# Four early transfers and two stores of a convolution with a maxout layer behind it, put in another place

## The chip, the cores and the metric

The kernel runs on one core of one Trainium2 chip. The metric is the device time of one execution in microseconds (us). A core has engines that work side by side, each through its own queue in order: PE (TensorE, matrix products; its weight loads are listed as PEld), DVE (VectorE), ACT (ScalarE), POOL (GpSimd) and SP (SyncE). Here POOL and SP mostly issue transfers (DMAs), which then run on 16 DMA engines without them. An instruction waits at the head of its engine's queue until the semaphores that it needs have come; everything behind it on that engine waits too.

## The reference

```python
def _attn_ref(x, weight_gen):            # x: 8 x 4160 x 192, weight_gen: 8 x 4160 x 8 x 7
    w = weight_gen - np.max(weight_gen, axis=-1, keepdims=True)
    w = np.exp(w)
    w = w / (np.sum(w, axis=-1, keepdims=True) + 1e-09)
    ...                                  # x_unf: at each position the last 7 rows of x, by head
    out = np.einsum('bshk,bskhg->bshg', w, x_unf)

def _moe_ref(x, w1, w2, w_out):          # x: 33280 x 192, d_ff 1024
    h1 = x @ w1
    h2 = x @ w2
    g = np.maximum(h1, h2)
    return (g @ w_out).astype(np.float32)
```

First a dynamic convolution over seven positions, whose taps are a softmax over seven numbers for each position and head; then, on its result, two products with 192 x 1024 weights, their maximum, and a product back to 192 columns.

## The kernel before, in words

**Tiling.** The 33,280 rows lie on 128 partitions, 260 consecutive rows (columns, in the code) on each. Columns are handled in batches of 16, and a last one of 4. A batch needs its logits (`load_wg`, 448 KB), its rows of x in two halves of 8 columns (`load_x`, 384 KB each as they are read) and, ahead of them, the last six columns of the batch before, its halo (`load_halo`, 288 KB, a copy from one x buffer to the other). There are two x buffers and four buffers of logits, used in turn, so batch 2 writes into the x buffer of batch 0.

**Steps of a batch.** ACT takes the exponential of the logits (`exp_sum`, line 162), DVE sums them (`red`, 180), ACT takes the logarithm (`ln`, 186), DVE subtracts it (`shift`, 191), and ACT takes the exponential again, which gives the taps in bf16 (`weights`, 202). DVE multiplies x and taps (`mul`, 218) and adds the seven products (`adds`, 244, 250, 253). The result is transposed: for batches 0 and 1 by PE with an identity (`sum_part`, line 307, copied out by ACT in line 316), from batch 2 on by a DMA that SP issues (`transpose`, 262). PE computes the hidden layer as a difference of the two products (`hid_tile`, 362), ACT applies the relu (`relu`, 372), PE multiplies by the output weights and adds the linear part (402 and 415), and ACT copies the results to `o_t` (`evac`, 487), from which SP stores them (501).

**What sets the order.** The schedule is written by hand: an instruction's place on its engine is where the program writes it. PE's work is cut into tiles of 1024 hidden numbers, in groups of two and, from tile 16 on, three; `hidden(g, ...)` writes one group, and the steps of the softmax and convolution are written between groups (the table `early` for groups 3 to 7, the tables `NOW` and `AT` afterwards). `behind(first, load)` makes a load wait for a named instruction, mostly the relu of a tile (`relu_of`) or a copy of a transposed unit (`yt_of`), so that it takes its place among the transfers: the first half of batch 2 waits for relu 8, the second half for relu 14, the first half of batch 3 for relu 16, the third logits for the copies of the linear part's weights (`w10_of`), the fourth for the copy of unit 4. From the first transposition by DMA on, POOL reads one element of the transposed tile (`gate`, 270), and the next loads stand behind that.

**Stores.** `evac` makes one store when a unit of columns is full. A unit is four columns in batches 0 and 1, eight afterwards. A store is either written at once or put into a list `held`, which is emptied ahead of a later store or behind the next transposition. In the kernel before, the stores of units 0, 1 and 2 are written at once and those from unit 3 on are held.

Of the kernel before, what the change touches and what calls it, by code (L numbers as in the profile page):

```python
# [17 lines left out]
def _sub(base: bass.AP, off: int, dims):  # L18
    ap = [list(base.ap[0])] + [[int(s), int(c)] for s, c in dims]
    return dataclasses.replace(base, offset=base.offset + off, ap=ap)  # L20
# [3 lines left out]
def kernel(  # L24
# [9 lines left out]
    nc = tc.nc  # L34
# [71 lines left out]
    def actual(v):  # L106
        return v + 8 if v < LAST - 8 else v - (LAST - 8) if v < LAST else v

    def load_wg(b, eng, o=0, n=None):
        c0, w = BATCHES[b]  # L110
        if b not in wg_ts:
            wg_ts[b] = pwg.tile([P, w * WGC], FP32, name="wg_t", tag="wg")
        parts = [(o, n)] if n else [(0, 8), (8, 8)] if c0 + w == LAST else [(0, w)]
        for o, n in parts:
            load = eng.dma_start(
                out=wg_ts[b][:, o * WGC:(o + n) * WGC],
                in_=bass.AP(tensor=weight_gen.tensor, offset=actual(c0 + o) * WGC,
                            ap=[[CPP * WGC, P], [1, n * WGC]]),
            )
        return load  # L120

    def x_at(b, o):

        c = BATCHES[b][0] + o
        key, at = (b, o) if c < LAST - 8 else ("wrap", 0) if c < LAST else (NB - 2, 8)
        if key not in xb_ts:
            xb_ts[key] = pxb.tile([P, (16 + PAD) * D], BF16, name="xb_t", tag="xb")
        return xb_ts[key], at * D

    def load_x(b, o, n, halo=True):  # L130

        t, at = x_at(b, o)
        load = nc.gpsimd.dma_start(  # L133
            out=t[:, at + PAD * D:at + (PAD + n) * D],
            in_=bass.AP(tensor=x.tensor, offset=actual(BATCHES[b][0] + o) * D,
                        ap=[[CPP * D, P], [1, n * D]]),
        )
        if 0 < b < NB - 1 and o == 0 and halo:
            load_halo(b)
        if "wrap" in xb_ts and t is xb_ts["wrap"]:  # L140
            nc.gpsimd.memset(t[0:1, 0:PAD * D], 0.0)
            nc.gpsimd.dma_start(
                out=t[1:P, 0:PAD * D],
                in_=bass.AP(tensor=x.tensor, offset=(CPP - PAD) * D, ap=[[CPP * D, P - 1], [1, PAD * D]]),
            )
        return load
# [5 lines left out]
    def load_halo(b):  # L152

        nc.gpsimd.dma_start(out=x_at(b, 0)[0][:, 0:PAD * D],
                            in_=xb_ts[b - 1][:, 16 * D:(16 + PAD) * D])
# [8 lines left out]
    def part(b, i, of):  # L164

        n = BATCHES[b][1]
        h0, h1 = n * i // of * H, n * (i + 1) // of * H
        return slice(h0, h1), h0 * K, [[K, h1 - h0], [1, K]]
# [4 lines left out]
    def sums(b, hs):  # L173

        at = BATCHES[b][0] * H - (0 if b < FIRST else s_parts[0].shape[-1])
        return s_parts[b >= FIRST][:, at + hs.start:at + hs.stop]

    def red(b, i=0, of=1):
        hs, at, ap = part(b, i, of)
        nc.vector.reduce_sum(out=sums(b, hs), in_=_sub(e_ts[b], at, ap), axis=AX.X)  # L180

    def ln(b, i=0, of=1):
        if i == 0:
            s_ts[b] = psm.tile([P, BATCHES[b][1] * H], FP32, name="ln_t", tag="ln")
        hs = part(b, i, of)[0]
        nc.scalar.activation(out=s_ts[b][:, hs], in_=sums(b, hs), func=AF.Ln)  # L186
# [7 lines left out]
    def weights(b, o):  # L194

        w = dict(pieces(b))[o]
        if b not in en_ts:
            en_ts[b] = pen.tile([P, 16 * WGC * 2], BF16, name="en_t", tag="en")
        J = 2 if w == 4 and b < 2 else 1
        N = w * H // J  # L200
        for j in range(J):
            nc.scalar.activation(  # L202
                out=_sub(en_ts[b], (o * WGC + j * N * K) * 2, [[2 * N, K], [2, N], [1, 2]]),
                in_=_sub(wg_ts[b], (o * H + j * N) * K, [[1, K], [K, N], [0, 2]]), func=AF.Exp,
            )
# [79 lines left out]
    def sum_transpose(u, taps=range(K), amid=lambda: None, now=True):  # L285

        copy = sum_part(u, 0, 3, taps)
        amid()
        sum_part(u, 3, 6, taps)
        if now:  # L290
            copy()
        return copy
# [30 lines left out]
    relu_of, yt_of, w10_of = {}, {}, []  # L323

    def behind(first, load):

        tc.add_manual_dep(load.ins, first.ins.name, SYNC, reason="its place among the transfers")
# [3 lines left out]
    held = []  # L331
# [43 lines left out]
    def column(c):  # L375

        b = min(c // 16, NB - 1)
        for u, (ub, o, n) in enumerate(UNITS):
            if ub == b and o <= c - BATCHES[b][0] < o + n:
                k = c - BATCHES[b][0] - o  # L380
                return u, k // 2, k % 2

    def place(p):

        u, i, _ = column(2 * p)
        b, o, n = UNITS[u]
        return BATCHES[b][0] + o + i, n // 2
# [82 lines left out]
    def evac(p, n):  # L470

        tile_, at = op_at[p]
        o = o_t[0]
        if p == NT // 2 - 1:

            for j, (copy, eng) in enumerate(((nc.scalar.copy, nc.scalar), (nc.vector.tensor_copy, nc.sync))):
                copy(out=o_last[:, j * D:(j + 1) * D], in_=tile_[:, at + 512 * j:at + 512 * j + D])  # L477
                eng.dma_start(
                    out=bass.AP(tensor=out.tensor, offset=actual(place(p)[0] + 2 * j) * D, ap=[[CPP * D, P], [1, D]]),
                    in_=o_last[:, j * D:(j + 1) * D],  # L480
                )
            return
        runs = [[q for q in range(p, p + n) if column(2 * q)[0] == u]
                for u in range(column(2 * p)[0], column(2 * (p + n - 1))[0] + 1)]
        for qs in runs:
            c, h = place(qs[0])
            nc.scalar.copy(out=_sub(o, c % 24 * D, [[D, len(qs)], [h * D, 2], [1, D]]),  # L487
                           in_=_sub(tile_, at + (qs[0] - p) * D, [[D, len(qs)], [512, 2], [1, D]]))
        stores = []
        for q in range(p, p + n):  # L490
            u, i, _ = column(2 * q)
            if NU - 7 <= u < NU - 1 and i % 2:
                stores.append((nc.sync, place(q)[0] - 1, [4 * D, 2], [1, 2 * D]))
            elif u < NU - 7 and i == UNITS[u][2] // 2 - 1:
                stores.append((nc.sync, place(q)[0] - i, [1, 2 * (i + 1) * D]))
            if u == NU - 1:
                stores.append((nc.sync, place(q)[0], [2 * D, 2], [1, D]))
        for eng, c, *ap in stores:

            def issue(eng=eng, c=c, ap=ap, o=o):  # L500
                eng.dma_start(
                    out=bass.AP(tensor=out.tensor, offset=actual(c) * D, ap=[[CPP * D, P], *ap]),
                    in_=_sub(o, c % 24 * D, ap),
                )

            if 3 <= u < NU - 3:
                held.append(issue)
            else:
                while u > 3 and held:
                    held.pop(0)()  # L510
                issue()

# [14 lines left out]
    NU = len(UNITS)  # L527
# [88 lines left out]
    with tc.tile_pool(name="pstage", bufs=1) as pstage:  # L616
# [148 lines left out]
        def w10_copies(pw):  # L765

            nc.scalar.copy(out=_sub(w10, 0, [[D, 2], [1, D]]), in_=_sub(pw, 0, [[512, 2], [1, D]]))
            for to, frm, at in ((64, 0, 0), (0, 64, 512)):
                w10_of.append(nc.scalar.copy(out=w10[to:to + 64, 2 * D:3 * D],
                                             in_=pw[frm:frm + 64, at:at + D]))  # L770
# [24 lines left out]
        relu(rd, 7, 1)  # L795
        weights(1, 8)
        w10_copies(pw)
        behind(w10_of[-1], load_wg(3, nc.gpsimd))
        load_halo(2)
        sum_transpose(3)  # L800
        out_first_weights(OUTS[3])
        adds(1, 4, True)
# [93 lines left out]
    none = lambda: None  # L896
# [7 lines left out]
    def rest_of_sum(u):  # L904
        sum_part(u, 3, 6, TAPS.get(u, range(K)))
        begun[u]()
# [1 line left out]
    early = {  # L908
        3: (none, rest_of_1),
        4: (lambda: (behind(relu_of[8], load_x(2, 0, 8, halo=False)),  # L910
                     rest_of_sum(4), behind(yt_of[4], load_wg(4, nc.gpsimd)), ln(2)), end_of_1),
        5: (lambda: (red(3), sum_transpose(5, LEFT), weights(2, 0)), none),
        6: (lambda: (weights(2, 8), ln(3), rest_of_sum(6)), none),
        7: (lambda: (behind(relu_of[14], load_x(2, 8, 8)), rest_of_sum(7)), none),
    }

    NOW = (22, 28, 40, 49, 106, 118)
# [122 lines left out]
```

## Time and profile before

| | |
|---|---|
| median of three runs | 411.82 us (410.1 to 411.96) |
| the profiled execution's own time | 409.58 us |
| its span | 407.8 us |
| granted PE clock, mean | 0.998 |
| DVE busy | 378.1 us, 231 instructions |
| PE busy | 397.4 us, 7370 products |
| ACT busy | 353.4 us, 418 instructions |
| POOL busy | 78.0 us, 108 instructions |
| moved by DMA | 66.32 MB, mean 163 GB/s |

The span is the stretch that the profile covers, and times in it count from its start. The rest of the profiled execution's time lies around it. An engine's busy time is what its instructions took; issuing a DMA isn't counted as busy on SP, and the time that a DMA takes from its issue to its landing is listed by itself. The chain of work that ended last is followed back from the last instruction, at each step to what released it, or to the instruction before it on its engine. Ends of PE's products are modelled, so that a busy PE isn't PE at its peak.

### The profile page before, as it was taken

How to read it: one execution, taken by the hardware profiler on the slowest of the kernel's cores; microseconds unless marked ns; L12 is line 12 of the kernel's file. 1: busy time of each engine (PE TensorE's matmuls, PEld its weight loads, DVE VectorE, ACT ScalarE, POOL GpSimd, SP SyncE). 2: the span in 40 equal slices, each digit the busy share in tenths (PEclk: the TensorE clock that was granted, in tenths of full speed). 3: DMA queues.
4: the chain of work that ended last, by engine and by line, in shares of the span. 5: the costliest groups of instructions: out<-in, count | busy, mean ns of one | idle time of the engine just before them, and what ended most of it. 6: DMA issues, size and time to landing. Idle time of an engine off the chain costs nothing.

```text
span 407.8 us, 16115 instructions
## 1 busy us (share of the span) xinstructions
PE 397.4 (97%) x7370; PEld 317.0 (78%) x7370; DVE 378.1 (93%) x231; ACT 353.4 (87%) x418; POOL 78.0 (19%) x108
## 2 busy tenths in 40 slices
PE   8899999999999999999999999999999999999994
PEld 3599999777777877777777787777777777877794
DVE  6999999999999999999999999999999999999500
ACT  3889999999999989998989999899998899897771
POOL 1421112122222201221211121222111223210000
PEclk9999999999999999999999999999999999999999
DMA  8988397756747675774785678577567567735313
GB/s 258 249 165 238 83 157 193 175 115 166 200 83 234 193 108 123 230 197 80 240 186 109 143 217 191 103 204 201 105 157 212 148 107 221 177 82 157 117 63 119
DMA packets 65110, 66.32 MB, mean 163 GB/s; under 512 B 49425, under 2 KB 54161, under 8 KB 65040
## 3 DMA queue, kind: packets, MB, share of 16 engines
q1 hardware_dynamic: 56064, 40.54, 36.1%
q0 software_dynamic: 8832, 24.63, 30.0%
q8 instruction: 58, 0.95, 0.9%
q10 hardware_dynamic: 144, 0.10, 0.1%
q14 instruction: 12, 0.10, 0.1%
HBM read 37.33 MB, written 25.56 MB: 154 GB/s over the span
## 4 chain that ended last, share of the span: by engine, by line
DVE 62%; PE 21%; ACT 9%; issue 4%; DMA 2%; POOL 0%; DVEq 0%; ACTq 0%; SPq 0%; POOLq 0%
DVE m_t L218 31%; DVE m_t L244 13%; DVE m_t L250 9%; PE op_ps L402 9%; PE hd L362 8%; ACT rd_t L372 5%; DVE y_t L253 3%; DVE s_rest L180 3%; DVE wg_t L191 2%; PE op_ps L415 2%; PE yps L307 1%; DMA yt<-y_t 1%; ACT yt L316 1%; ACT en_t L202 1%; PE hdp L362 1%
## 5 line engine op out<-in xcount | busy, mean ns | idle before, releaser
L372 ACT ACTIVATE rd_t<-hd 128x1024 bf16<-128x1024 f32 (+1 forms) x206 | 234.4, 1187 | 26.3 <-PE hd L362 25.0
L402 PE MATMUL op_ps<-wo,rd_t 64*128 64x192 bf16 x4160 | 210.8, 243 | 0.0
L402 PEld LDWEIGHTS <-rd_t 64*128 64x128 bf16 x4160 | 181.1, 94 | 15.5
L362 PE MATMUL hd<-yt,wd 64*128 64x512 bf16 (+1 forms) x1584 | 187.4, 360 | 0.5 <-ACT rd_t L372 0.4
L218 DVE TENSOR_TENSOR m_t<-xb_t,en_t 128x10752 bf16<-128x10752 bf16 (+1 forms) x35 | 181.6, 5193 | 0.0
L362 PEld LDWEIGHTS <-wd 64*128 64x128 bf16 x1776 | 94.4, 94 | 44.2 <-issue 3.5
L270 POOL CAST gate<-yt 128x1 f32<-128x1 bf16 x29 | 39.0, 1343 | 262.9 <-DMA yt<-y_t 262.9
L244 DVE TENSOR_TENSOR m_t<-m_t 128x4608 bf16<-128x4608 bf16 (+1 forms) x31 | 75.6, 2438 | 0.1
L487 ACT COPY o_t<-op_ps 128x384 f32<-128x384 f32 (+1 forms) x99 | 57.2, 588 | 12.3 <-PE op_ps L402 12.3
L415 PE MATMUL op_ps<-w,yt 64*128 64x192 bf16 x768 | 54.7, 243 | 0.1
L415 PEld LDWEIGHTS <-yt 64*128 64x128 bf16 x768 | 37.9, 94 | 16.4 <-issue 1.3
L250 DVE TENSOR_TENSOR m_t<-m_t 128x3072 bf16<-128x3072 bf16 (+1 forms) x29 | 50.1, 1727 | 0.1
L202 ACT ACTIVATE en_t<-wg_t 128x896 bf16<-128x896 f32 (+2 forms) x45 | 35.9, 820 | 0.7 <-DVE wg_t L191 0.7
L253 DVE TENSOR_TENSOR y_t<-m_t 128x1536 bf16<-128x1536 bf16 (+1 forms) x29 | 27.3, 943 | 0.5
L133 POOL DMA_DIRECT2D xb_t<-in_x_dram x34 | 18.2, 536 | 30.9 <-ACT rd_t L372 20.5
L191 DVE TENSOR_TENSOR wg_t<-wg_t,ln_t 128x280 f32<-128x280 f32 (+5 forms) x46 | 22.2, 483 | 0.4 <-ACT ln_t L186 0.3
L372 ACT ACTIVATE rd_t<-hdp 128x1024 bf16<-128x1024 f32 x16 | 16.1, 1030 | 1.4 <-PE hdp L362 1.4
L162 ACT ACTIVATE e_t<-wg_t 128x896 f32<-128x896 f32 (+2 forms) x18 | 16.2, 900 | 1.3 <-DMA wg_t<-in_weight_gen_dram 1.3
L477 DVE COPY o_last<-op_ps 128x192 f32<-128x192 f32 x1 | 0.4, 357 | 18.0 <-ACT o_last L477 18.0
L180 DVE TENSOR_REDUCE s_rest<-e_t 128x64 f32<-128x448 f32 (+2 forms) x27 | 16.4, 609 | 0.0
L362 PE MATMUL hdp<-yt,wd 64*128 64x256 bf16 x192 | 14.0, 270 | 2.0 <-ACT rd_t L372 1.6
L307 PE MATMUL yps<-ident,m_t 64*128 64x64 bf16 x600 | 11.8, 190 | 0.7 <-ACT yt L316 0.4
(53 smaller groups left out, 89.1 us busy)
## 6 DMA issues: line engine op xcount, KB each, us to landing
out_dram<-o_t SPq DMA_DIRECT2D x22, 768.0 KB, 5.3
xb_t<-in_x_dram POOLq DMA_DIRECT2D x30, 384.0 KB, 4.8
out_dram<-o_t SPq DMA_DIRECT2D x20, 384.0 KB, 3.2
wg_t<-in_weight_gen_dram POOLq DMA_DIRECT2D x13, 448.0 KB, 5.3
xb_t<-xb_t POOLq DMA_DIRECT2D x15, 288.0 KB, 5.0
xb_t<-in_x_dram POOLq DMA_DIRECT2D x4, 192.0 KB, 5.2
xs<-in_x_dram SPq DMA_DIRECT2D x1, 576.0 KB, 4.0
ws0E<-in_moe_w_dram SPq DMA_DIRECT2D x2, 256.0 KB, 5.3
```

The costliest lines, as they stand in the source:

```text
L191: nc.vector.tensor_tensor(out=w_t, in0=w_t, in1=_sub(s_ts[b], hs.start, [[1, hs.stop - hs.start], [0, K]]), op=ALU.subtract)
L202: nc.scalar.activation(out=_sub(en_ts[b], (o * WGC + j * N * K) * 2, [[2 * N, K], [2, N], [1, 2]]), in_=_sub(wg_ts[b], (o * H + j * N) * K ...
L218: return nc.vector.tensor_tensor(out=m_out, in0=x_in, in1=_sub(en_ts[b], o * WGC * 2, [[2, K * n * H], [0, G // 2], [1, 2]]), op=ALU.mult,)
L244: nc.vector.tensor_tensor(out=taps(0, 1, 3), in0=taps(0, 1, 3), in1=taps(3, 1, 3), op=ALU.add)
L250: nc.vector.tensor_tensor(out=taps(0, 2, 2), in0=taps(0, 2, 2), in1=taps(1, 5, 2), op=ALU.add)
L253: nc.vector.tensor_tensor(out=_sub(y_ts[b], o * D, [[64, 2], [P, 3 * w // 2], [1, 64]]), in0=taps(0, 1, 1), in1=taps(2, 1, 1), op=ALU.add,)
L270: nc.gpsimd.tensor_copy(out=gate, in_=yt[:, 0:1])
L362: nc.tensor.matmul(hid_out(t, f, j), lhsT=wd_at(j, s, f // 4, f % 4 * P, P), rhs=_sub(yt_ts[u][half(j), :], (s + j) % 3 * P, [[3 * P, w // ...
L372: relu_of[t0] = nc.scalar.activation(out=rd[:, k * 1024:(k + n) * 1024], in_=hd[:, at:at + n * 1024], func=AF.Relu)
L402: return nc.tensor.matmul(op_out(c), lhsT=rd[half(r), k * 1024 + at:k * 1024 + at + P], rhs=wo[half(r), f * D:(f + 1) * D], start=start, s ...
L415: nc.tensor.matmul(op_out(c + j), lhsT=yt_ts[u][half(j), (3 * i + (s + j) % 3) * P:(3 * i + (s + j) % 3 + 1) * P], rhs=w10[half(j), s * D: ...
L487: nc.scalar.copy(out=_sub(o, c % 24 * D, [[D, len(qs)], [h * D, 2], [1, D]]), in_=_sub(tile_, at + (qs[0] - p) * D, [[D, len(qs)], [512, 2 ...
```

## The change

Three things are edited. In `evac` the stores of units 0 and 1 are held too, and the list is emptied ahead of the store of unit 2, so that the three are written one behind the other. The halo copy of batch 2 is written ahead of the load of the third logits in place of behind it. The load of the fourth logits moves from group 4, behind the copy of unit 4, to group 7, behind relu 14; the second half of batch 2, which was behind relu 14, is now ahead of it and behind relu 13.

```diff
@@ evac
-            if 3 <= u < NU - 3:
+            if u < 2 or 3 <= u < NU - 3:
                 held.append(issue)
             else:
-                while u > 3 and held:
+                while u > 1 and held:
                     held.pop(0)()
                 issue()
@@
         w10_copies(pw)
+        load_halo(2)
         behind(w10_of[-1], load_wg(3, nc.gpsimd))
-        load_halo(2)
         sum_transpose(3)
@@ early
         4: (lambda: (behind(relu_of[8], load_x(2, 0, 8, halo=False)),
-                     rest_of_sum(4), behind(yt_of[4], load_wg(4, nc.gpsimd)), ln(2)), end_of_1),
+                     rest_of_sum(4), ln(2)), end_of_1),
         5: (lambda: (red(3), sum_transpose(5, LEFT), weights(2, 0)), none),
         6: (lambda: (weights(2, 8), ln(3), rest_of_sum(6)), none),
-        7: (lambda: (behind(relu_of[14], load_x(2, 8, 8)), rest_of_sum(7)), none),
+        7: (lambda: (behind(relu_of[13], load_x(2, 8, 8)), behind(relu_of[14], load_wg(4, nc.gpsimd)),
+                     rest_of_sum(7)), none),
```

## The prediction

> **What bounds the kernel now.** I read first the page's busy times and its chain of work that ended last, then a table of busy times by stage, then the order in time of POOL, SP, DVE and ACT around the transfers that the change touches. The page's first rows and its chain by engine:
>
> ```profile
> span 407.8 us, 16115 instructions
> ...
> PE 397.4 (97%) x7370; PEld 317.0 (78%) x7370; DVE 378.1 (93%) x231; ACT 353.4 (87%) x418; POOL 78.0 (19%) x108
> ...
> DVE 62%; PE 21%; ACT 9%; issue 4%; DMA 2%; POOL 0%; DVEq 0%; ACTq 0%; SPq 0%; POOLq 0%
> ```
>
> The table by stage has the stretch in us from the span's start, its length, then busy time of PE, PEld, DVE, ACT and POOL, the granted clock, the DMA share and GB/s:
>
> ```profile
> 20.00:30.00 10.00, 9.45 (x307) 8.70 (x305) 10.00 (x5) 8.56 (x18) 1.61 (x3) 1.00 0.92 176
> 30.00:40.00 10.00, 9.94 (x309) 9.42 (x304) 9.96 (x7) 10.00 (x16) 1.61 (x3) 1.00 0.78 215
> 40.00:50.00 10.00, 9.54 (x287) 9.06 (x281) 10.00 (x5) 9.09 (x13) 0.78 (x2) 1.00 0.40 83
> 50.00:60.00 10.00, 10.00 (x218) 9.96 (x215) 10.00 (x8) 9.71 (x12) 1.97 (x5) 1.00 0.96 178
> ...
> 90.00:370.00 280.00, 279.94 (x4858) 218.25 (x4856) 279.51 (x154) 253.40 (x283) 58.92 (x71) 1.00 0.67 161
> ```
>
> The reader is to see the third busy column, DVE: 39.96 us of the 40 from 20 to 60, and 279.51 of 280 from 90 to 370. DVE doesn't wait for a transfer anywhere in the stretch that the change touches. DMA holds 2% of the chain that ended last. So there is no DMA wait in this execution that an earlier transfer could remove; the change can only add one, or remove one that this execution doesn't show.
>
> **The transfers that move.** In the order in time of POOL (start, duration, what is issued, and in brackets the idle time before it and what ended it):
>
> ```profile
> 22.14 0.53 POOL L133 DMA_DIRECT2D xb_t<-in_x_dram  x1 [4.34 <-ACT rd_t L372]
> ...
> 29.42 0.54 POOL L115 DMA_DIRECT2D wg_t<-in_weight_gen_dram  x1 [5.82 <-ACT w L769]
> 30.04 0.54 POOL L154 DMA_DIRECT2D xb_t<-xb_t  x1
> ...
> 35.90 0.54 POOL L115 DMA_DIRECT2D wg_t<-in_weight_gen_dram  x1 [1.45 <-ACT ln_t L186]
> 45.73 0.54 POOL L133 DMA_DIRECT2D xb_t<-in_x_dram  x1 [9.29 <-ACT rd_t L372]
> 49.76 0.53 POOL L133 DMA_DIRECT2D xb_t<-in_x_dram  x1 [3.49 <-ACT rd_t L372]
> 51.04 0.54 POOL L154 DMA_DIRECT2D xb_t<-xb_t  x1 [0.75 <-DMA xb_t<-in_x_dram]
> ```
>
> These are, in order: the second half of batch 1; the third weights; the halo copy of batch 2; the fourth weights; the second half of batch 2; the first half of batch 3; its halo copy. Their consumers, in the order in time of DVE and ACT:
>
> ```profile
> 21.53 8.69 DVE L218 TENSOR_TENSOR m_t<-xb_t,en_t 128x5376 bf16<-128x5376 bf16 x3
> ...
> 41.52 5.75 DVE L218 TENSOR_TENSOR m_t<-xb_t,en_t 128x10752 bf16<-128x10752 bf16 x1
> ...
> 53.33 5.75 DVE L218 TENSOR_TENSOR m_t<-xb_t,en_t 128x10752 bf16<-128x10752 bf16 x1
> 59.00 0.62 DVE L180 TENSOR_REDUCE s_rest<-e_t 128x64 f32<-128x448 f32 x1
> ```
>
> ```profile
> 36.63 0.94 ACT L162 ACTIVATE e_t<-wg_t 128x896 f32<-128x896 f32 x1
> ...
> 40.36 1.96 ACT L372 ACTIVATE rd_t<-hdp 128x1024 bf16<-128x1024 f32 x2
> ...
> 44.38 1.05 ACT L372 ACTIVATE rd_t<-hdp 128x1024 bf16<-128x1024 f32 x1
> ...
> 55.04 0.98 ACT L162 ACTIVATE e_t<-wg_t 128x896 f32<-128x896 f32 x1
> ```
>
> The product at 41.52 needs the halo of batch 2, the one at 53.33 its second half. The exponentials at 36.63 and 55.04 need the third and the fourth weights. How long transfers take from issue to landing: the first row is all loads of weights issued from 18 to 62 us, the second all loads and copies into the x buffers there, the third all stores up to 120, the last the single load issued at 45.73 (shortest, median, longest):
>
> ```profile
> DMA to landing us min/median/max: 4.0/5.3/6.2
> ```
>
> ```profile
> DMA to landing us min/median/max: 4.1/4.8/5.0
> ```
>
> ```profile
> DMA to landing us min/median/max: 2.3/4.4/7.1
> ```
>
> ```profile
> L133 POOL DMA_DIRECT2D xb_t<-in_x_dram x1: 537/537/537, 45.7 to 45.7; - x1
> ...
> DMA to landing us min/median/max: 5.0/5.0/5.0
> ```
>
> And how full the DMA engines are (the same columns as the table above; the share is the next to last):
>
> ```profile
> 28.00:30.00 2.00, 1.73 (x96) 1.61 (x94) 2.00 (x1) 1.32 (x5) 0.54 (x1) 1.00 0.05 15
> 42.00:46.00 4.00, 3.64 (x120) 3.31 (x113) 4.00 (x1) 3.66 (x7) 0.27 (x1) 1.00 0.02 4
> 48.00:56.00 8.00, 8.00 (x173) 7.96 (x170) 8.00 (x6) 7.28 (x10) 1.08 (x2) 1.00 0.95 195
> ```
>
> **The change part by part.** PE, DVE and ACT have the same instructions in the same order in both programs, nothing is added or taken away. Only what four POOL issues wait for, and their order, differ.
>
> *The stores.* SP's rows are
>
> ```profile
> 31.30 16.23 SPq L501 DMA_DIRECT2D out_dram<-o_t  x3
> ```
>
> ```profile
> L501 SPq DMA_DIRECT2D out_dram<-o_t x2: 332/335/338, 38.9 to 47.2; - x2
> ```
>
> so the three stores go at 31.3, 38.9 and 47.2, each behind the copy on ACT that fills its part of `o_t`. The edit writes the first two down later in the program, but nothing else stands on SP between them and the third: SP's instructions keep their order, and each store still waits for the same count of ACT's instructions. I take 0; SP issues them when it did. A loss would need them really held until 47.2; that is priced below.
>
> *The halo copy of batch 2 ahead of the third weights.* It needs the second half of batch 1, landed by 22.14 + 5.0 = 27.1, and the end of batch 0's last product, the first of the three from 21.53, at 21.53 + 8.69/3 = 24.4. With the 0.3 us from landing to issue (51.04 against 45.73 + 5.0 = 50.73 for the next halo) it goes at about 27.4 in place of 30.04; POOL is free again at 27.9, before the third weights' own wait ends at 29.42. So these leave at 29.42 as before, and land by 29.42 + 6.2 = 35.6, 1.0 ahead of 36.63. Most of the copy's time before 29.42 falls into a stretch, from 28 to 30, whose DMA share is 0.05. No gain: it was landed by 30.04 + 5.0 = 35.0 and is needed at 41.52. Loss: if the weights' bytes started only when the copy has landed (27.4 + 5.0 = 32.4), they would land 4.0 to 6.2 later, at 36.4 to 38.6, so 0 to 2.0 late. I take 0, since the shares of the engines are nearest to the first case. [...]
>
> *The second half of batch 2.* It waits for relu 13, the second of the two at 40.36, which ends at 42.32, in place of relu 14, at 44.38 + 1.05 = 45.43. With the same 0.30 us to the issue (45.73 less 45.43) it goes at 42.6 in place of 45.73, 3.1 us earlier, into a stretch with a DMA share of 0.02, and lands by 47.6. Its product starts at 53.33: the slack grows from 53.33 - 50.73 = 2.6 us to 5.7. Gain in this execution: 0, as DVE doesn't wait. Loss: none, it overtakes only the fourth weights.
>
> *The fourth weights.* They take that place behind relu 14: 45.73 in place of 35.90. The next issue behind them on POOL waits for a relu until 49.76, so their 0.54 us of issue delay nobody. They land 4.0 to 6.2 later, at 49.7 to 51.9, and are needed at 55.04: slack 3.1 to 5.3, where it was 12.9 to 15.1. Their cover is DVE's two products' time and ACT's relus; if it's gone, ACT waits with the exponential, the relu behind it makes PE wait, and from 59.00 DVE too. They join the fullest stretch. By bytes: 448 KB of weights, the store at 47.2 (384), batch 3's half (384) and its halo (288) are 1,504 KB, 1.54 MB; at 195 GB/s that is 7.9 us, so even served last they are there at 45.73 + 0.54 + 7.9 = 54.2, 0.9 before the exponential. I take 0.
>
> Sum: 0 + 0 + 0 + 0. Against the profiled execution's own 409.58 us the sum is 409.58. The median of the runs shown is 411.82, 2.24 above it, with runs from 410.1 to 411.96; I predict the median, **411.8 us**.
>
> **The rivals.**
>
> *A hidden stall goes away (faster).* The runs without a profile were up to 2.4 us longer than the profiled one, and something in them may wait. The tightest load that goes straight into DVE, the bound, is the second half of batch 2 with 2.6 us. If it came 2.24 us behind its consumer in those runs, the change, which adds 3.1 us, removes all of it: 409.6. For it: the slack is among the smallest. Against it: it would have to land 4.8 us later than in the trace (2.6 of slack and 2.24), where the loads and copies into the x buffers differ by 0.9 (4.1 to 5.0), and the same 2.24 us can lie in anything else.
>
> *The fourth weights come late (slower).* The place is the exponential at 55.04. With one store's worth of traffic it isn't reached (54.2). If the two early stores were really held to 47.2, 768 KB join: 2,272 KB, 2.33 MB, 11.9 us at 195 GB/s, landing at 58.2, 3.2 us late. ACT has 0.3 us idle in ten there and PE none, so I carry it through whole: 411.8 + 3.2 = 415.0. It decides, by over 0.5%, once they land past 57.1, that is 11.4 us after issue; the longest of all rows above is 7.1. [...]
>
> *The third weights behind the halo.* Up to 2.0 us on the exponential at 36.63, worked out above: 411.8 to 413.8, mostly inside what can't be told from no change.
>
> *The store edit works as it is named* is the second rival's condition; read by itself it does nothing.
>
> **How the numbers follow.** About 0.5%, 2 us, is what a measurement of this kernel can tell from no change. Likeliest, no transfer late: 0.66, its own range 410.1 to 413. Hidden stall removed: 0.14, all of it faster. Fourth weights late: 0.12, nearly all of it slower. Third weights late: 0.08, of it 0.01 beyond 2 us. So faster 0.14, same 0.73, slower 0.13. The range takes in the faster rival's 409.6 with a little beside it and the third rival's 413.8, and leaves out most of the second: 409.3 to 414.0.
>
> **What would show it.** Right: on POOL the halo copy at 27 to 28, the third weights still at 29.4, batch 2's second half at 42.6, the fourth weights at 45.7; on SP stores at 31.3, 38.9 and 47.2; DVE busy 10 of 10 us from 20 to 60; the exponentials at 36.6 and 55.0. Wrong: an idle ACT before either exponential that a weight load ended, an idle DVE before its products at 41.5 or 53.3, or three stores together at 47. If the spans agree and the times don't, the cause lies where no trace shows it.

## The result

The changed kernel takes 410.53 us (median of 22 runs, 409.91 to 412.89) against 411.81 for the kernel before (22 runs beside them, 410.1 to 412.61): a ratio of 0.9976, with a 95% interval from 0.9966 to 0.9986. So about 1 us went, a quarter of a per cent. The forecast of 411.8 lies 1.3 us too high, within its range and within the half per cent that was called no change. The value came out nearly right; the reason given for it did not: the forecast is the median of the kernel before with all four terms put at 0, and the runs below show that two of them are not 0.

From the page of the changed kernel (its first row, the busy times, the chain that ended last by engine):

```profile
span 408.5 us, 16115 instructions
...
PE 397.1 (97%) x7370; PEld 316.7 (78%) x7370; DVE 378.3 (93%) x231; ACT 353.6 (87%) x418; POOL 79.1 (19%) x108
...
PE 69%; DVE 18%; ACT 7%; DMA 3%; issue 1%; POOL 0%; SPq 0%; DVEq 0%; ACTq 0%; POOLq 0%
```

The chain is PE's for 69%, where it was DVE's for 62% before. This profiled execution took 410.31 us, the one of before 409.58, which is below all 22 of that kernel's runs. The two profiles can therefore not simply be subtracted: the one of before shows an unusually good execution, and what the change takes away is hardly in it.

POOL's issues in the order of time, from the halo copy on:

```profile
28.52 0.54 POOL L154 DMA_DIRECT2D xb_t<-xb_t  x1 [4.46 <-DMA xb_t<-in_x_dram]
29.89 0.54 POOL L115 DMA_DIRECT2D wg_t<-in_weight_gen_dram  x1 [0.82 <-ACT w L769]
33.94 0.54 POOL L133 DMA_DIRECT2D xb_t<-in_x_dram  x1 [3.51 <-ACT rd_t L372]
43.12 0.53 POOL L133 DMA_DIRECT2D xb_t<-in_x_dram  x1 [8.64 <-ACT rd_t L372]
46.24 0.54 POOL L115 DMA_DIRECT2D wg_t<-in_weight_gen_dram  x1 [2.58 <-ACT rd_t L372]
```

and SP's stores (three issues in one row, from the first to the end of the last):

```profile
31.32 16.72 SPq L501 DMA_DIRECT2D out_dram<-o_t  x3
```

The moves are the forecast ones, half a microsecond later because this execution starts later (DVE waits for a load of x at the start and is 0.47 us behind from there on); the halo copy alone is 1.1 us later than forecast. The stores stand where they stood, the third with the same half microsecond.

### The profile page after: what moved, and what is told of

It is laid out like the page before. It is cut to its first block, busy times and chain, and to the rows that moved or that the text cites. A ratio compares the mean times of both kernels' runs of the same rounds, so it can differ in the third digit from the quotient of the medians.

```text
span 408.5 us, 16115 instructions
## 1 busy us (share of the span) xinstructions
PE 397.1 (97%) x7370; PEld 316.7 (78%) x7370; DVE 378.3 (93%) x231; ACT 353.6 (87%) x418; POOL 79.1 (19%) x108
## 4 chain that ended last, share of the span: by engine, by line
PE 69%; DVE 18%; ACT 7%; DMA 3%; issue 1%; POOL 0%; SPq 0%; DVEq 0%; ACTq 0%; POOLq 0%
PE op_ps L402 31%; PE hd L362 29%; DVE m_t L218 8%; PE op_ps L415 6%; ACT rd_t L372 4%; DVE m_t L244 4%; DVE m_t L250 3%; PE hdp L362 2%; PE yps L307 1%; DMA xs<-in_x_dram 1%; DVE y_t L253 1%; DMA yt<-y_t 1%; DMA xb_t<-in_x_dram 1%; DVE m_t L227 1%; ACT en_t L202 1%
## 5 line engine op out<-in xcount | busy, mean ns | idle before, releaser
L270 POOL CAST gate<-yt 128x1 f32<-128x1 bf16 x29 | 40.2, 1385 | 262.6 <-DMA yt<-y_t 262.6
L415 PEld LDWEIGHTS <-yt 64*128 64x128 bf16 x768 | 37.8, 94 | 16.8 <-issue 1.7
```

The lines of the kernel that those rows point to most:

```text
L270: nc.gpsimd.tensor_copy(out=gate, in_=yt[:, 0:1])
L415: nc.tensor.matmul(op_out(c + j), lhsT=yt_ts[u][half(j), (3 * i + (s + j) % 3) * P:(3 * i + (s + j) % 3 + 1) * P], rhs=w10[half(j), s * D: ...
```

## The experiments

**What was looked for.** DVE waits for no moved transfer in either profile. Three theories: A, the second half of batch 2, the load with the least slack, comes late in ordinary executions; B, what counts is the crowd of transfers around 30 to 36; and, after the first four runs, F, PE waits for its own instructions, which are themselves brought by DMA. Each ratio is to runs of the kernel before made beside the run.

**One part at a time.** The stores alone:

```diff
-            if 3 <= u < NU - 3:
+            if u < 2 or 3 <= u < NU - 3:
...
-                while u > 3 and held:
+                while u > 1 and held:
```

> Only the first two stores are written down later; every transfer keeps its place and its waits. Both theories: ratio 1.000 within 0.1%, median about 411.8 us, and runs scattered as those of the kernel before are (410.1 to 412.6), so that the profile likely catches an execution of 411 to 412.5 us and shows which wait the fast profile of before lacked. If instead it is 1 us faster, the store edit does something that SP's order doesn't show.

Measured: 411.91 us, ratio 1.0002 (0.9987 to 1.0018). The store edit does nothing. Since this is the old schedule in all else, its profile (411.93 us) is one of a usual execution of the kernel before, and it is used as such below.

The halo copy alone:

```diff
+        load_halo(2)
         behind(w10_of[-1], load_wg(3, nc.gpsimd))
-        load_halo(2)
```

> Only the halo copy of batch 2 is ahead of the third weights. Theory A (the gain of 1.3 us comes from the second half of batch 2 leaving before the full stretch from 46 us): ratio 1.000, median 411.8. Theory B (it comes from the copy's leaving the stretch from 30 to 36 us, where it stands beside the third weights and the first store): the whole gain, ratio about 0.9975, median 410.5.

Measured: 411.17 us, 0.9985 (0.9973 to 0.9997).

The fourth weights and batch 2's second half together:

```diff
-                     rest_of_sum(4), behind(yt_of[4], load_wg(4, nc.gpsimd)), ln(2)), end_of_1),
+                     rest_of_sum(4), ln(2)), end_of_1),
...
-        7: (lambda: (behind(relu_of[14], load_x(2, 8, 8)), rest_of_sum(7)), none),
+        7: (lambda: (behind(relu_of[13], load_x(2, 8, 8)), behind(relu_of[14], load_wg(4, nc.gpsimd)), rest_of_sum(7)), none),
```

> Only the second half of batch 2 goes to relu 13 and the fourth weights to relu 14. Theory A: the whole gain, ratio about 0.9975, median 410.5. Theory B: 1.000, median 411.8.

Measured: 411.11 us, 0.9982 (0.9968 to 0.9995).

Batch 2's second half alone, behind relu 13, with the fourth weights left at their old place:

```diff
-        7: (lambda: (behind(relu_of[14], load_x(2, 8, 8)), rest_of_sum(7)), none),
+        7: (lambda: (behind(relu_of[13], load_x(2, 8, 8)), rest_of_sum(7)), none),
```

> Only the second half of batch 2 goes to relu 13 (42.6 us in place of 45.7); the fourth weights stay at 35.9. Theory A: the whole gain, ratio about 0.9975. If the fourth weights' leaving the stretch from 36 to 41 us is what counts, 1.000 here and 0.9975 with both moved. Theory B: 1.000.

Measured: 412.02 us, 1.0004 (0.9991 to 1.0018). Theory A falls: the load with the least slack, 3 us earlier, is worth nothing. Theory B, which gave the halo copy the whole gain and the other two moves none, doesn't hold either: each has a part. The fourth weights weren't moved by themselves, so their part is a difference: 0.9982 with both loads moved, 1.0004 with batch 2's second half alone. What counts is that the fourth weights no longer leave at 36 and, about as much, that the halo copy no longer leaves at 30. The two parts add up to 0.33% against 0.24% for the whole change, which agree within their intervals of 0.10 to 0.14% to either side. Nothing that DVE or ACT was seen to wait for is among them.

**Where the time is.** PE's rows of the stores-only run, in the order of time, show four stops inside groups of products that depend on nothing new; "issue" is time in which the engine waited for nothing that the profile shows:

```profile
28.31 0.38 PE L307 MATMUL yps<-ident,m_t 64*128 64x64 bf16 x13
29.31 1.21 PE L307 MATMUL yps<-ident,m_t 64*128 64x64 bf16 x71 [0.62 <-issue]
30.34 0.67 PE L457 MATMUL op_ps<-w,yt 64*128 64x192 bf16 x12
...
32.40 0.34 PE L307 MATMUL yps<-ident,m_t 64*128 64x64 bf16 x11
33.04 0.62 PE L307 MATMUL yps<-ident,m_t 64*128 64x64 bf16 x31 [0.30 <-issue]
33.49 0.83 PE L362 MATMUL hdp<-yt,wd 64*128 64x256 bf16 x12
...
36.32 0.57 PE L402 MATMUL op_ps<-wo,rd_t 64*128 64x192 bf16 x9
37.59 0.49 PE L402 MATMUL op_ps<-wo,rd_t 64*128 64x192 bf16 x7 [0.69 <-issue]
37.85 0.88 PE L362 MATMUL hdp<-yt,wd 64*128 64x256 bf16 x12
...
41.44 0.35 PE L307 MATMUL yps<-ident,m_t 64*128 64x64 bf16 x11
42.41 0.62 PE L307 MATMUL yps<-ident,m_t 64*128 64x64 bf16 x31 [0.61 <-issue]
42.87 0.82 PE L362 MATMUL hdp<-yt,wd 64*128 64x256 bf16 x12
```

The groups of 84, 42, 16 and 42 products are broken after 13, 11, 9 and 11. Between two stops stand 71 + 12 + 12 + 6 + 16 + 11 = 128 products, and the same for the others; with the weight load of each product, that is 256 instructions of PE. The same groups of the changed kernel are whole, each with the row behind it:

```profile
28.35 1.40 PE L307 MATMUL yps<-ident,m_t 64*128 64x64 bf16 x84
29.58 0.66 PE L457 MATMUL op_ps<-w,yt 64*128 64x192 bf16 x12
...
31.64 0.78 PE L307 MATMUL yps<-ident,m_t 64*128 64x64 bf16 x42
32.25 0.82 PE L362 MATMUL hdp<-yt,wd 64*128 64x256 bf16 x12
...
35.23 1.20 PE L402 MATMUL op_ps<-wo,rd_t 64*128 64x192 bf16 x16
36.20 0.88 PE L362 MATMUL hdp<-yt,wd 64*128 64x256 bf16 x12
...
40.28 0.83 PE L307 MATMUL yps<-ident,m_t 64*128 64x64 bf16 x42
40.94 0.82 PE L362 MATMUL hdp<-yt,wd 64*128 64x256 bf16 x12
```

From a group's start to the next row's start it is 1.23, 0.61, 0.97 and 0.66 us here, and 2.03, 1.09, 1.53 and 1.43 in the stores-only run. The shortest that any profile has for these groups is 1.23, 0.61, 0.66 and 0.61; what goes beyond that is called the loss below. It finds short stops too that aren't listed as one, such as the 0.31 us in the third group here. That the first two groups are whole here is in part luck: the eleven other profiles in the table further below lose 0.42 us or more at 29, and one of them is a second profile of the changed kernel.

The page's list of DMA queues has two for instructions (packets, MB, share of 16 engines), with the same packets and bytes in all profiles:

```profile
q8 instruction: 58, 0.95, 0.9%
...
q14 instruction: 12, 0.10, 0.1%
```

58 packets of 0.95 MB are 16.4 KB each; PE's 7,370 products and as many weight loads, divided by 58, are 254 instructions for one. So the theory: PE gets its instructions in blocks of 256 through the same DMA engines as the data (the page gives q8 0.9% of the 16 engines' span), shortly ahead of their use. In the stores-only run the packets of q8 begin at 30.4, 35.3, 40.1 and 43.5, that is 1.0, 2.2, 2.5 and 1.1 us after PE began the block before (29.31, 33.04, 37.59, 42.41); at its stops PE goes on 2.3 to 2.7 us after a packet's start. The late ones are those of 35.3 and 40.1, in the traffic of the halo copy with batch 2's first half and of the fourth weights. The one of 30.4 isn't late but long, 1.30 us where the next two take 0.93 and 1.03. In the changed kernel the packets begin at 29.1, 33.3, 37.8 and 41.6, 0.6, 1.5, 1.8 and 1.1 us after the block before.

The records of all thirteen profiles agree with this. Between 22 and 50 us two like products of PE begin over 0.25 us apart 37 times, each time where a block of 128 products ends, and PE goes on 1.26 to 1.60 us after the end of that block's packet, whether the packet took 0.88 or 1.81 us. No block of any profile begins sooner than 1.13 us after its packet's end.

**Where the blocks end.** If the stops lie at block ends, then four dummy products fewer at the program's start move every stop by four products:

```diff
-        keep_warm(18)
+        keep_warm(14)
```

> The kernel before with four of the first 18 warming products left out, so that everything behind them on PE stands 8 instructions earlier in its stream; no transfer moves. Theory F (PE's stops without a named releaser are at the ends of blocks of 256 of its instructions, 128 weight loads with their products, whose next block a DMA brings late): the stops that split a transposition's 42 products as 11 and 31 now split them as 15 and 27, and the one that split 16 output products as 9 and 7 splits them as 13 and 3; time within 0.2% of before. Rival R (PE waits at these places for data, which the profile doesn't name): the stops stay at the same products, 11 and 31, 9 and 7.

Measured: 411.8 us, 1.0008 (0.9996 to 1.0021), and the group of 42 is broken after 15 in place of 11:

```profile
40.20 0.41 PE L307 MATMUL yps<-ident,m_t 64*128 64x64 bf16 x15
40.79 0.56 PE L307 MATMUL yps<-ident,m_t 64*128 64x64 bf16 x27 [0.17 <-issue]
```

The other two of its stops moved by four as well (17 and 67 products, 13 and 3). That the stops belong to blocks of 256 instructions is shown, and rival R is not seen.

**The fourth weights at their old place again,** in the changed kernel, as a second, needless load:

```diff
-                     rest_of_sum(4), ln(2)), end_of_1),
+                     rest_of_sum(4), behind(yt_of[4], load_wg(4, nc.gpsimd)), ln(2)), end_of_1),
```

> The changed kernel with one transfer added: the fourth weights are also loaded at their old place behind the copy of unit 4 (then again behind relu 14, same data). Every load that a consumer needs is there as early as in the changed kernel. Theory F: the traffic from 36 to 41 us is back, and with it the stop of PE at about 42 us (as in e2, 0.3 to 0.6 us), so the median is 0.4 to 1.0 us above the changed kernel's, 411.0 to 411.5, ratio to before 0.9980 to 0.9990. Rival A (a tight load came late before): no change against the changed kernel, 410.5, 0.9970 to 0.9976.

Measured: 410.67 us, 0.9980 (0.9970 to 0.9990). In the profile the stop at 42 is back, and longer:

```profile
42.16 0.62 PE L307 MATMUL yps<-ident,m_t 64*128 64x64 bf16 x31 [0.89 <-issue]
```

But the profiled execution, 411.85 us, is the slowest of its 12 runs. The median lies below the 411.0 to 411.5 that F expected; the ratio is at the fast end of F's range, and its interval takes in the rival's as well as the changed kernel's 0.9976. The trace speaks for F, the times don't decide.

**The stores really held,** by a wait of the first two for the third's copy, in the kernel before (together with the store edit above) and in the changed one. The added lines are the same:

```diff
-            nc.scalar.copy(out=_sub(o, c % 24 * D, ...
+            copied = nc.scalar.copy(out=_sub(o, c % 24 * D, ...
...
-                eng.dma_start(
+                return eng.dma_start(
...
-                    held.pop(0)()
+                    store = held.pop(0)()
+                    if u == 2:
+                        behind(copied, store)
```

> The kernel before, its first two stores now made to wait for the copy that fills the third (about 47 us), so that 768 KB leave the stretch from 31 to 43 us and join the one from 47 on. Theory F: the stop at about 37.6 us goes, the others shrink, the median falls by 0.6 to 1.5 us to 410.4 to 411.3, ratio 0.9963 to 0.9985. My prediction's second rival (traffic from 47 us on makes the fourth weights or batch 2's second half late): 412 to 415.

> The changed kernel, its first two stores made to wait for the third's copy as well. Theory F: what stops are left in its slower runs go, median 410.0 to 410.5, ratio to before 0.9955 to 0.9970. The second rival of the prediction: the fourth weights share the stretch from 46 us with three stores, and by its sum land at 58.2, 3.2 us behind their exponential: 411 to 414, with ACT idle ahead of that exponential.

In the kernel before: 410.54 us, 0.9982 (0.9971 to 0.9993), and the three stores leave together:

```profile
48.05 1.42 SPq L501 DMA_DIRECT2D out_dram<-o_t  x3
```

There is no stop at 37, and no load is late; time and ratio are in F's range. In the changed kernel: 411.01 us, 0.9993 (0.9979 to 1.0008), where F expected 410.0 to 410.5. That was a miss. The rival's time, 411 to 414, is just reached, but not by its cause: in the profile, 410.32 us, the fourth weights leave at 46.53 and land 4.8 us later, 4.5 ahead of their exponential at 55.84, and ACT doesn't wait for them. It has one listed stop (0.53 at 29.05), so why its other runs are longer isn't known.

**Which engine has nothing to spare.** The changed kernel once more, beside two kernels with a little more work at about 33 to 37, on PE and on DVE:

> The changed kernel once more, beside the two that follow. Expected by the reading so far (PE stops for its own instructions, and the change takes most of these stops away): 410.3 to 410.9, 0.9966 to 0.9986 of the kernel before. If the difference seen first was chance: 0.999 or above.

```diff
         sum_part(u, 3, 6, taps)
+        if u == 3:
+            sum_part(u, 3, 6, taps)
```

> The changed kernel with 42 products of the third unit's transposition (its second half) done twice, so that they are overwritten with the same numbers: by the rows of such groups of 42, where the next row starts 0.61 to 0.65 us later, 0.6 to 0.65 us more for PE at about 33, nothing more for any other engine. If PE has no time to spare from there on, as the stops' cost needs: 0.4 to 0.7 us longer than the changed kernel of the same call (about 0.0013 of the time more). If DVE alone is the bound, as the prediction had it: 0.

```diff
     def rest_of_1():
         mul(1, 8)
         red(2)
+        red(2)
```

> The changed kernel with the sum of batch 2's exponentials done twice on DVE, 1.08 us more there at about 37, nothing more for PE, ACT or POOL. If DVE is the bound in this stretch, as the prediction had it: 1.0 to 1.1 us longer than the changed kernel of the same call. If PE alone is: 0. If both are full, so that a delay of either goes through to the end: 1.0 to 1.1 here and 0.4 to 0.7 in the run with more products.

The expectation of the kernel with more products has them overwritten; in fact they add up, and that half of unit 3 comes out doubled. That changes the numbers, not the work, which is 42 products more. Measured: the changed kernel 411.0 us, 0.9975 (0.9965 to 0.9984), the same gain a second time; with 0.61 us more on PE 411.96, 1.0002 (0.9990 to 1.0013); with 1.12 us more on DVE 411.51, 0.9992 (0.9982 to 1.0003). More work on PE costs 0.96 us against the changed kernel beside it (0.2 to 1.4 by resampling the runs), more work on DVE 0.5 (0.3 to 0.9). Neither fits what was written down: 0.4 to 0.7 for PE, and for DVE 1.0 to 1.1 or 0. The 0.96 isn't the price of the products alone, because the blocks also end elsewhere. DVE's delay isn't free, but only a part of it goes through: in that profile PE waits 0.71 us for ACT at 40.93. So these two times don't name the bound; the rows further below do. The 42 products put in also move the next stop as the count of 128 says, 113 + 12 + 3:

```profile
28.79 1.82 PE L309 MATMUL yps<-ident,m_t 64*128 64x64 bf16 x113 [0.19 <-issue]
...
32.79 0.70 PE L364 MATMUL hdp<-yt,wd 64*128 64x256 bf16 x9 [1.48 <-issue]
```

**PE from 49 us on, in all runs.** From unit 7's last transposed group on PE hardly stops: in the stores-only run it is busy for 353.22 of the 353.80 us from 48.7 on. The last transposed group of unit 7 and the last group of products of the whole program, in the stores-only run:

```profile
48.65 0.53 PE L307 MATMUL yps<-ident,m_t 64*128 64x64 bf16 x24
...
402.55 2.16 PE L402 MATMUL op_ps<-wo,rd_t 64*128 64x192 bf16 x48
```

and in the changed kernel:

```profile
46.73 0.53 PE L307 MATMUL yps<-ident,m_t 64*128 64x64 bf16 x24
...
400.85 2.16 PE L402 MATMUL op_ps<-wo,rd_t 64*128 64x192 bf16 x48
```

Between these two rows lie 353.90 and 354.12 us. In all thirteen profiles it is 353.88 to 354.12. DVE has no such constant. Its product on the second half of batch 2, in the stores-only run, the changed kernel and the one with more DVE work:

```profile
53.95 5.75 DVE L218 TENSOR_TENSOR m_t<-xb_t,en_t 128x10752 bf16<-128x10752 bf16 x1
```

```profile
53.80 5.75 DVE L218 TENSOR_TENSOR m_t<-xb_t,en_t 128x10752 bf16<-128x10752 bf16 x1
```

```profile
55.36 5.75 DVE L218 TENSOR_TENSOR m_t<-xb_t,en_t 128x10752 bf16<-128x10752 bf16 x1
```

From there to PE's last group it is 348.60, 347.05 and 346.78 us: up to 1.8 us of DVE's place in time don't show at the end. So the time is decided before 49 us, by when PE has finished the early stage. The table gives for each profile the start of the group of 84, the losses in the four places, the start of unit 7's last group, and the execution's own time:

| run | halo copy / fourth weights | 84-group | loss at 29 | at 33 | at 37 | at 42 | unit 7 | own time |
|---|---|---|---|---|---|---|---|---|
| before | late / early | 27.88 | 0.45 | 0.20 | 0.05 | 0.02 | 46.22 | 409.58 |
| stores only | late / early | 28.31 | 0.80 | 0.48 | 0.87 | 0.82 | 48.65 | 411.93 |
| x only | late / early | 28.63 | 0.51 | 0.20 | 0.87 | 1.09 | 48.67 | 411.96 |
| blocks shifted | late / early | 28.03 | 0.50 | 0.20 | 0.49 | 0.37 | 46.95 | 410.35 |
| stores held, before | late / early | 28.07 | 0.52 | 0.20 | 0.05 | 0.57 | 47.02 | 410.54 |
| swap only | late / late | 28.54 | 0.59 | 0.48 | 0.87 | 0 | 47.90 | 411.44 |
| halo only | early / early | 27.84 | 0.76 | 0.48 | 0 | 0.52 | 47.03 | 410.52 |
| weights twice | early / early | 28.16 | 0.42 | 0.48 | 0.87 | 1.09 | 48.40 | 411.85 |
| after | early / late | 28.35 | 0 | 0 | 0.31 | 0.05 | 46.73 | 410.31 |
| stores held, after | early / late | 28.15 | 0.71 | 0.20 | 0 | 0.29 | 47.02 | 410.32 |
| after again | early / late | 28.75 | 1.45 | 0.48 | 0 | 0.01 | 48.13 | 411.90 |
| more DVE | early / late | 28.72 | 0.42 | 0.76 | 0.05 | 0 | 48.25 | 411.60 |

The reader is to see the two columns at 37 and 42. At 42 PE loses 0.64 us on average of the seven profiles with the fourth weights early, and 0.07 in the five with them late. At 37 it loses 0.53 on average of the six with the halo copy late, and 0.21 in the six with it early. Together 0.90 us, beside the 1.0 to 1.3 that the timed runs show.

These are averages of single profiles, and the rows overlap: 0.05 twice at 37 with the copy late, 0.87 once with it early. The losses at 29 and 33 come and go with either, and so does the start; a single profile can be worse than the one of another schedule by them alone, as the changed kernel's second profile is. The loss at 29 can't be the change's: the packet behind it begins at 26.2 to 28.0 us, at 24.7 in the first profile of the changed kernel, ahead of every transfer that moves.

The execution's own time is the start of unit 7's group plus 363.3 to 363.8 us in all twelve rows, and that start follows from the columns ahead of it. Unit 7's group less the start of the 84-group, less the four losses, is 17.4 to 17.7 us in all rows but two: 18.0 in the changed kernel, where PE also waited 0.28 us for ACT at 39.38, and 18.3 with more DVE work, where it waited those 0.71. What the moved transfers can have changed is thus the losses from 33 on. That they did is shown by the timed runs of the parts and by this account; which loss went by how much is known from these few profiles alone.

With more products the blocks end elsewhere, so that run isn't in the table. Its own time, 410.76 us, is below all its other runs, although PE was the latest of all (48.91 and 402.80): its last two stores took 1.8 and 1.9 us where all others took 3.3 to 4.0.

```profile
out_dram<-o_last ACTq DMA_DIRECT2D x1, 96.0 KB, 1.9
...
out_dram<-o_last SPq DMA_DIRECT2D x1, 96.0 KB, 1.8
```

## Why the prediction was right, and where it was wrong

*What bounds the kernel.* This step failed: "DVE, the bound". The row quoted for it, of 90 to 370 us, has 279.51 us of DVE and, two columns to its left, 279.94 of PE; the page's first row has PE at 97% and DVE at 93%. The stage that the change touches was read on DVE's column alone, where PE's 9.45, 9.94 and 9.54 of 10 were there to be read as losses. Both engines are full later on; PE is the one that can't make up what it lost. The constant 353.9 us shows it, beside 346.8 to 348.6 from DVE's product to the same row. The runs with more work on PE and on DVE fit it (0.96 us for 0.61; 0.5 for 1.12) but would not show it alone.

*"The change can only add one, or remove one that this execution doesn't show."* The second half of that sentence is what happened: PE lost 0.72 us in the four groups of that profile, and 2.97 in the stores-only run of the same schedule. The 2.24 us between the profiled execution and the median was named and left unexplained. Between these two profiles it is 411.93 less 409.58, 2.35 us, and unit 7's last group already starts 2.43 later; the losses are 2.25 of that and the later start 0.43, with 0.25 won back between.

*The stores at 0.* Right: SP's row and the run of that part alone, 1.0002.

*The halo copy.* The size 0 was wrong: it is worth 0.15%. The forecast time, 27.4, was 1.1 us early. Half of that is this execution's later start; the rest is in two of its terms. The second half of batch 1 took 5.3 us to land where 5.0 were taken (22.61 + 5.3 = 27.9), and the copy went 0.6 us behind that landing where 0.3 were taken. Its row names this landing; the product of batch 0 that the prediction has it wait for had ended at 24.9 (22.00 + 8.69/3).

*The third weights* left at 29.89 and landed in 3.4 us, far from late: the rival that had them wait for the whole halo copy isn't seen.

*Batch 2's second half.* Right in time (42.6 forecast, 43.12 with the later start) and in worth: 0, by the run of this part alone.

*The fourth weights.* Right in time (45.7 and 46.24) and in the cover: they landed 3.6 us later, at 49.8, and the exponential stood at 55.55. The size 0 was wrong again, with about 0.2% by the difference of two runs: nothing was asked of what else moved where they had been. All four terms were priced by the wait of a consumer, and the cost that moved was that of a bystander, PE waiting for its own instructions.

*The rivals.* A hidden stall did go away, in that rival's direction and by a little over half its size (1.3 of 2.24 us), but not at its place: batch 2's half was not the load. The fourth weights were not late even with the stores really held: the changed kernel with that, 411.01, was far from the rival's 415, and the weights had 4.5 us to spare.

*The value.* Two zeros in place of gains of 0.15 and about 0.2% leave a forecast within 0.31% all the same. It was near because the terms that were missed are small, not because the reason held: that is luck. Nothing in the prediction's sum could have given their size.

## What to carry to other kernels

Read every engine's column in the stage that is changed, and take as the bound the one that can't catch up later: a constant time from one of its rows to the end, over several executions in which the other engine's varies, names it (here 353.88 to 354.12 us from PE's row in all thirteen profiles, 346.78 to 348.60 from DVE's in three). A stop with "issue" as its releaser in the middle of a group of like products, a multiple of 128 products with their weight loads away from the next, was PE waiting for its own instructions here (0.30 to 0.69 us at each of the four in the stores-only run), and transfers that nobody waited for had a part in it (0.15% for the halo copy, about 0.2% for the fourth weights). When a single profiled execution is faster than all timed runs (409.58 us here, beside 410.1 and more), what the others lose isn't in it; take another profile of the same schedule before a zero is believed.

## What the runs showed of the hardware

By their number the 58 packets of q8 bring PE's instructions, 16.4 KB or 254 instructions each. Its stops stood 128 products with their weight loads apart, that is 256 instructions, and moved by four products when four were left out ahead of them. In the stores-only run, where PE ran 128 products in 3.4 to 4.2 us (its stops taken off), packets began as late as 2.5 us after the block before, and PE stopped for 0.30 to 0.69 us at the blocks' ends; in the run with more products one stop took 1.48 us. At its stops PE went on 1.26 to 1.60 us after the packet's end.

It isn't shown whether a packet waits for other transfers, or for which: the late ones fall into the traffic of the halo copy and the fourth weights, but that rests on the table and on when the packets begin. The one at 37 begins 2.0 to 2.4 us after the block before in four of the six profiles with the copy late and 1.3 and 1.5 in two; with it early, 1.1 to 1.5 in five of the table's six and 2.3 in one. The one at 42 begins 1.8 to 2.7 us after it in the seven with the fourth weights early, and 1.1 to 2.1 in the five with them late. Why the changed kernel with the stores really held is slower in most runs than in its profile, and why the second load of the fourth weights costs no time in its median, is open too.
